# A planner that tells float32 matmul groups from float16 ones, and a first batch planned anew

## The chip, the core and the metric

One core of a Trainium2 chip runs the kernel. The metric is the device time of one execution in microseconds (us); each kernel is given by the median of several executions.

## What is computed

Attention within hash buckets, then a gated two-matrix layer (4 batches, 8 heads, 768 positions, head size 64; 512 model columns, 1536 hidden columns):

```python
q_bits = einsum('bhsd,dk->bhsk', q, proj) > 0      # 6 bits for each query, and for each key
mask   = q_bucket[..., :, None] == k_bucket[..., None, :]
scores = where(mask, q @ k.T / 8, -1e9)
attn   = softmax(scores)
x      = (attn @ v) laid out as (3072, 512)
out    = ((x @ w_a) * (x @ w_b)) @ w_out
```

## The kernel before

**The pieces.** The work is cut into batch `b`, chunk of 256 queries `c` (3 for each batch) and `half` of the heads. Each of these 24 units has eight score tiles. A name such as `s_2_1_0_1_1_0` reads: batch 2, chunk 1, half 0, then head pair, head and row tile. TensorE works in groups of matmuls, and the groups carry the names of the tiles that they write:

- `s` (L740): four matmuls of 384 columns on float32 (fp32r) operands; the scores of one tile, in one of two PSUM buffers with tag `s`. VectorE takes the row maximum `mx` (L752) and adds a constant (`bias`, L759), ScalarE takes the exponent `e` (L767), and with that the PSUM buffer is free.
- `av` (L801): 18 matmuls of 64 columns on float16; weights times values, once the float16 halves `a2` of `e` (L781 on VectorE, L786 on GpSimd) have been transposed by DMA into `at`.
- `px` (L837): four transposes of the normalized output `x` (L828), which then becomes float16 `xT0` (ScalarE, L848) and `xT1` (VectorE, L851).
- `ab` (L885): twelve matmuls of 256 columns on float16; `x @ w_a` or `x @ w_b` for 128 hidden columns. Two such groups fill the one `ab` buffer; ScalarE (`a`, L899) and VectorE (`g`, L907) empty it, and ScalarE and GpSimd split the product into two float32 parts (L914, L917).
- `o` (L927): six matmuls of 512 columns on float32; the product times `w_out`.
- `pk`, `kb`, `ko` and `pq`, `qb`, `qo`: the preparation of keys and of queries: transposes, bit sums (`kb` and `qb` are float32, L513), and bit differences (float16).

**Float32 groups** below are `s`, `o`, `kb` and `qb`; all other groups are called float16 groups, the transposes among them.

**Who sets the order.** Every piece is recorded as an operation of a `Plan` with an engine, a duration in us, a key (its due time in score tiles) and the tiles that it reads and writes. `Plan.issue` then steps through a time of its own: an engine that is free takes, among the operations whose inputs and buffers are there, the one with the lowest key. The instructions are written out in that order, and on the chip each engine runs its own list in order, waiting on semaphores. The choice, at L181:

```python
for o in ready[e]:
    if o.ready <= now and (best is None or (o.key, o.seq) < (best.key, best.seq)) and can(o):
        best = o
```

The keys of batch 0 are tables at the head (L42 to L52): when keys, values and queries are loaded, when the weights `w_a`, `w_b` (`WG0`) and `w_out` (`WO0`) are brought into shape (`raw`, `wab`, `wo_y`, `wo`), and when the first two units of the second layer start (`M0`, `M0_PACE`). Later batches repeat one pattern: 16 score tiles for each 12 rounds of `ab`, `ab`, `o`.

Of the kernel before, what the change touches and what calls it, by code (L numbers as in the profile page):

```python
# [31 lines left out]
NCH = S // CH  # L32
TPC = CH // P

NE, NA, NAT, NO = 3, 2, 2, 2

ACT_CASTS = 8
K_LEAD, Q_LEAD, V_LEAD = 8.0, 2.5, 6.0  # L42
M_LAG = 7.0
K0 = [-12.0, -11.5, -9.5, 6.0]
V0 = [-2.0, -2.0, 5.5, 0.5]
Q0 = [-6.0, 4.5, 9.0, 14.0, 29.0, 31.5]
VS0 = -3.0
WG0 = [11.0, 7.0, 11.5, 14.0, 17.5, 23.5]
S_LAG = -2.5
WO0 = [13.5, 16.0, 36.0]  # L50
M0 = [19.0, 42.5]
M0_PACE = [1.88, 1.33]  # L52
BIG = float(2.0**60)
ESC = float(2.0**14)
# [31 lines left out]
DVE_BESIDE, POOL_BESIDE = 0.5, 0.25  # L86


class Buf:


# [10 lines left out]


class Op:
    __slots__ = ("eng", "dur", "fn", "key", "bufs", "svc", "sbuf", "preds", "succs", "npred", "ready", "seq")


class Plan:
# [4 lines left out]
    def __init__(self):  # L113
        self.ops, self.writer, self.readers = [], {}, {}

    def op(self, eng, dur, fn, key, r=(), w=(), svc=0.0, hold=(), sbuf=False):
        o = Op()
        o.eng, o.dur, o.fn, o.key, o.svc, o.sbuf = eng, dur, fn, key, svc, sbuf
        o.seq = len(self.ops)
        preds = set()  # L120
        for x in r:
            if x in self.writer:
                preds.add(self.writer[x])
            self.readers.setdefault(x, []).append(o.seq)
        for x in w:
            if x in self.writer:
                preds.add(self.writer[x])
            preds.update(self.readers.pop(x, ()))
            self.writer[x] = o.seq
        preds.discard(o.seq)  # L130
        o.preds = preds
        o.bufs = []
        for x in (*r, *w, *hold):
            x = x[0] if isinstance(x, tuple) else x
            if isinstance(x, Buf) and x not in o.bufs:
                o.bufs.append(x)
                x.left += 1
        self.ops.append(o)
        return o

    def issue(self):
# [7 lines left out]
        ready = {e: [] for e in free}  # L149
# [3 lines left out]
        live = {}  # L153
        dma_free = 0.0
        held = set()
        beside = False
        done = 0
        now = 0.0
        events = [0.0]
# [10 lines left out]
        while done < len(ops):  # L170
# [6 lines left out]
            for e in free:  # L177
                if free[e] > now:
                    continue
                best = None  # L180
                for o in ready[e]:  # L181
                    if o.ready <= now and (best is None or (o.key, o.seq) < (best.key, best.seq)) and can(o):
                        best = o
                if best is None:
                    continue
                o = best
# [8 lines left out]
                if e == "DVE":  # L195
                    beside = o.sbuf
                    if o.sbuf and free["POOL"] > now:
                        end += DVE_BESIDE
                elif e == "POOL" and beside and free["DVE"] > now:
                    end += POOL_BESIDE  # L200
                free[e] = end
# [28 lines left out]
def attention_moe(ctx: ExitStack, tc: tile.TileContext, q, k, v, proj, w_a, w_b, w_out, cst, cst_w, out):  # L230
# [288 lines left out]
    def kprep(b, hp, key, tag):  # L519
# [49 lines left out]
        def rows():  # L569
# [2 lines left out]
                bit_rows(psb.t[:, j, :HALF], [(h, tr[h].t[:, 1, cols]) for h in range(2)], exact)  # L572

        op(
            "PE", 1.5 if exact else 0.75, rows, key,
            r=["pjw"] + [(tr[h], x) for h in range(2) for x in ("hi2", "lo")], w=[psb],
        )
        if exact:
            op(
# [26 lines left out]
                    start=True, stop=True,  # L606
                )

        op("PE", 0.35, diffs, key, r=["bits_k", "wbit"], w=[pso])
        for h in range(2):  # L610
            op(
                "ACT", 0.81,
# [7 lines left out]
    def qprep(b, c, half, key, tag):  # L620
# [30 lines left out]
        for h in range(2):  # L651
# [23 lines left out]
                psb.t[:, 0, :CH],  # L675
                [(2 * j + h, trq[h].t[:, j, 1, :]) for j in range(2) for h in range(2)], exact,
            ),
            key, r=["pjw"] + [(trq[h], x) for h in range(2) for x in ("hi2", "lo")], w=[psb],
        )
        if exact:  # L680
            op(
# [25 lines left out]
                    start=True, stop=True,  # L707
                )

        op("PE", 0.25, diffs, key, r=["bits_q", "wbit"], w=[pso])  # L710
        for h in range(2):
            op(
                "ACT", 0.68,
# [7 lines left out]
    def su_state(b, c, half):  # L721
        n = f"{b}_{c}_{half}"
        return dict(
            mx=buf("mx", [P, 4 * TPC], F32, f"mx_{n}", 3),
            bias=buf("bias", [P, 4 * TPC], F32, f"bias_{n}", 3),
            sm=buf("sm", [P, 4 * TPC], F32, f"sm_{n}", 3),
            av=buf("av", [P, 4 * TPC, D], F32, f"av_{n}", 1, pp),
        )

    def qtile(b, c, half, j, h, t, st, key):  # L730
# [6 lines left out]
        def scores():  # L737
# [5 lines left out]
                    )  # L743

        op(
            "PE", 0.72, scores, key, w=[ps],
            r=[(trq, x) for x in ("hi", "hi2", "lo", "hot")] + [(tr, x) for x in ("hi", "hi2", "lo", "pen")],
        )
        mx, bias, sm, av = st["mx"], st["bias"], st["sm"], st["av"]
        op(  # L750
# [58 lines left out]
    def su_end(b, c, half, st, key, tag):  # L809
# [34 lines left out]
        def part(y):  # L844
            return y.t[:, 2 * half : 2 * half + 2, :].rearrange("p j s -> p (j s)")

        op("PE", 0.45, tps, key, r=[x, "csb"], w=[ps], hold=[hi, lo])
        op("ACT", 0.6, lambda: nc.scalar.copy(out=part(hi), in_=ps.t[:, 0]), key, r=[ps], w=[(hi, half)])  # L848
        op(
            "DVE", 0.68,  # L850
# [7 lines left out]
    def moe(b, c, key, pace, alone):  # L858
# [3 lines left out]
        for f in range(NF):  # L862
# [16 lines left out]
            for m in range(2):  # L879

                def first(m=m, f=f, pl=pl):
                    i = 0
                    for wi, xi in ((0, xh), (1, xh), (0, xl)):
                        for cc in range(NC):
                            nc.tensor.matmul(  # L885
                                pl.t[:, m, :CH], lhsT=wt(m, wi, cc, f), rhs=xi.t[:, cc, :],
                                start=i == 0, stop=i == 3 * NC - 1,
                            )
                            i += 1

                j0 = (gr + m) * NC
                op(
                    "PE", 1.31, first, kf, w=[(pl, m)],
                    r=xtok + [(x, j0 + cc) for x in "WL" for cc in range(NC)],
                )
            a = buf("a", [P, CH], F32, f"a_{n}", 1)
# [26 lines left out]
            def second(f=f, g=g):  # L923
# [6 lines left out]
                        )  # L930

            op(
                "PE", 1.42, second, kf + pace * 1.2, w=[po],
                r=[g[0], g[1], (wo[f], 0), (wo[f], 1)],
            )
        for u in range(TPC):
# [83 lines left out]
```

## Time and profile before

| | |
|---|---|
| median of 3 runs | 1012.32 us (1007.96 to 1012.86) |
| the profiled execution | 1012.15 us, of which the span takes 1010.4 us |
| busy: TensorE matmul, weight loads | 936.4 us (93%), 793.3 us (79%) |
| busy: VectorE, ScalarE, GpSimd | 630.5 us (62%), 557.5 us (55%), 456.2 us (45%) |
| chain that ended last, by engine | TensorE 86%, VectorE 7%, ScalarE 3%, issue 2%, DMA 1% |
| chain that ended last, by line | `ab` 37%, `o` 19%, `s` 13%, `av` 9% |

The profile is of one execution. "Busy" counts an engine's instructions; the chain is followed back from the last instruction, at each step to what released it or to the instruction before it on its engine. In the chain view, a row's time runs up to the start of the next row, so that it is the time that a group took of the engine.

### The profile page before, as it was taken

To read this page: it belongs to the slowest core of one execution; us is meant where nothing else is said; L and a number is where in the kernel's file an instruction comes from. 1 tells how busy PE (TensorE), PEld (TensorE's weight loads), DVE (VectorE), ACT (ScalarE), POOL (GpSimd) and SP (SyncE) were. 2 spreads that over 40 slices of the span, in tenths; PEclk is the share of its full clock that TensorE was granted. 3 is DMA by queue.
4 is the path that set the end of the run, shared out by engine and by line. 5 is a ranking of instruction groups with operands and counts; after the bars stand their busy time and mean duration, and the time that the engine had idled before them with its cause. 6 is when DMAs were issued, how large, how long until landed. Compare 5 with 4: busy or idle time off the path is not lost.

```text
span 1010.4 us, 22786 instructions
## 1 busy us (share of the span) xinstructions
PE 936.4 (93%) x9132; PEld 793.3 (79%) x9132; DVE 630.5 (62%) x1135; ACT 557.5 (55%) x1067; POOL 456.2 (45%) x372
## 2 busy tenths in 40 slices
PE   3464679999999999999999999999999999999998
PEld 1243468888888888888888888888888888888886
DVE  4798998777575555567676565557666565555111
ACT  5888865645655554455665555455665554443221
POOL 1033345446554555544555555544545455455211
PEclk9856779999999999999999999999999999999999
DMA  8589956666555445566544565465554455544100
GB/s 286 223 213 208 188 127 139 123 165 149 102 124 116 105 101 131 110 131 152 119 128 106 105 127 109 108 149 137 126 123 103 105 133 103 95 101 95 32 22 21
DMA packets 370154, 127.46 MB, mean 126 GB/s; under 512 B 353920, under 2 KB 362368, under 8 KB 370048
## 3 DMA queue, kind: packets, MB, share of 16 engines
q1 hardware_dynamic: 370048, 126.00, 54.9%
q8 instruction: 72, 1.18, 0.5%
q14 instruction: 34, 0.28, 0.1%
HBM read 44.18 MB, written 6.29 MB: 50 GB/s over the span
## 4 chain that ended last, share of the span: by engine, by line
PE 86%; DVE 7%; ACT 3%; issue 2%; DMA 1%; SPq 0%; POOL 0%; POOLq 0%; DVEq 0%; ACTq 0%
PE ab L885 37%; PE o L927 19%; PE s L740 13%; PE av L801 9%; PE kb L513 2%; PE qb L513 2%; DVE mx L752 1%; PE pk L539 1%; PE px L837 1%; PE pq L644 1%; ACT e L767 1%; DVE wab L370 1%; DVE wab L425 1%; DVE trk L560 1%; PE ko L604 1%
## 5 line engine op out<-in xcount | busy, mean ns | idle before, releaser
L786 POOL TENSOR_TENSOR a<-e,a 128x768 f16<-128x768 f32 x192 | 323.2, 1683 | 322.0 <-DVE a L781 175.9
L885 PE MATMUL ab<-xT,wab 128*128 128x256 f16 x3456 | 413.3, 273 | 0.5 <-DVE bias L759 0.5
L885 PEld LDWEIGHTS <-wab 128*128 128x128 f16 x3456 | 326.4, 98 | 59.4 <-issue 23.3
L767 ACT ACTIVATE e<-s,bias 128x768 f32<-128x768 f32 x192 | 172.7, 899 | 136.5 <-DVE bias L759 125.1
L927 PE MATMUL o<-wo,g 128*128 128x512 f32 x864 | 234.3, 406 | 0.3 <-ACT g L914 0.2
L752 DVE TENSOR_REDUCE mx<-s 128x1 f32<-128x768 f32 x192 | 182.5, 951 | 70.1 <-PE s L740 69.2
L917 POOL TENSOR_TENSOR g<-g,g 128x256 fp32r<-128x256 f32 x144 | 109.0, 757 | 186.1 <-ACT g L914 175.2
L740 PE MATMUL s<-trk,trq 128*128 128x384 f32 x768 | 180.5, 365 | 7.8 <-ACT e L767 6.3
L927 PEld LDWEIGHTS o<-wo,g 128*128 128x128 f32 x864 | 153.4, 189 | 27.6 <-ACT g L914 0.7
L907 DVE SCALAR_TENSOR_TENSOR g<-ab,absc,a 128x256 f32<-128x256 f32 x144 | 69.4, 482 | 158.8 <-ACT a L899 147.1
L801 PEld LDWEIGHTS <-at 128*128 128x128 f16 x3456 | 122.7, 100 | 32.7 <-issue 24.0
L740 PEld LDWEIGHTS s<-trk,trq 128*128 128x128 f32 x768 | 135.5, 198 | 15.7 <-ACT e L767 10.5
L899 ACT ACTIVATE a<-ab,absc 128x256 f32<-128x256 f32 x144 | 68.3, 474 | 131.0 <-PE ab L885 129.9
L801 PE MATMUL av<-vh,at 128*128 128x64 f16 x2304 | 133.8, 196 | 4.8 <-DMA at<-a 4.8
L781 DVE CAST a<-e 128x768 f16<-128x768 f32 x184 | 111.5, 606 | 25.7 <-ACT e L767 19.6
L914 ACT CAST g<-g 128x256 fp32r<-128x256 f32 x144 | 58.1, 404 | 55.9 <-DVE g L907 54.1
L801 PE MATMUL av<-vl,at 128*128 128x64 f16 x1152 | 66.6, 195 | 1.8 <-DVE vl L499 1.8
L714 ACT ACTIVATE trq<-qo,csb 64x512 fp32r<-64x512 f32 x48 | 32.8, 683 | 35.4 <-PE qo L705 34.9
L664 DVE TENSOR_TENSOR trq<-pq,trq 64x512 fp32r<-64x512 f32 x48 | 33.0, 688 | 24.2 <-ACT trq L659 20.7
L555 POOL CAST trk<-trk 64x768 fp32r<-64x768 f32 x32 | 26.7, 833 | 40.3 <-ACT trk L548 39.4
L560 DVE SCALAR_TENSOR_TENSOR trk<-pk,trk 64x768 fp32r<-64x768 f32 x32 | 30.6, 955 | 21.7 <-ACT trk L548 21.2
L654 ACT CAST trq<-pq 64x512 fp32r<-64x512 f32 x48 | 27.8, 580 | 23.0 <-PE pq L644 20.0
(77 smaller groups left out, 670.9 us busy)
## 6 DMA issues: line engine op xcount, KB each, us to landing
rk<-in_k_dram SPq DMA_DIRECT2D x32, 192.0 KB, 3.2
raw_w<-in_moe_w_b_dram SPq DMA_DIRECT2D x12, 512.0 KB, 6.4
raw_w<-in_moe_w_a_dram SPq DMA_DIRECT2D x12, 512.0 KB, 8.2
raw_wo<-in_moe_w_out_dram SPq DMA_DIRECT2D x12, 512.0 KB, 5.3
rq<-in_q_dram SPq DMA_DIRECT2D x96, 64.0 KB, 2.4
vm<-in_v_dram SPq DMA_DIRECT2D x16, 384.0 KB, 3.5
vr<-in_v_dram SPq DMA_DIRECT2D x16, 384.0 KB, 3.6
out_dram<-osb SPq DMA_DIRECT2D x24, 256.0 KB, 2.7
```

Source lines behind the costliest of these rows:

```text
L740: nc.tensor.matmul(ps.t[:, jj, :HALF], lhsT=trq.t[:, j, i, t * P : (t + 1) * P], rhs=tr.t[:, i, jj * HALF : (jj + 1) * HALF], start=i == 0 ...
L752: lambda: nc.vector.tensor_reduce(out=mx.t[:, u : u + 1], in_=halves(ps.t), axis=AX.XY, op=ALU.max, negate=True),
L767: lambda: nc.scalar.activation(flat2(e.t), halves(ps.t), AF.Exp, bias=bias.t[:, u : u + 1], scale=1.0, accum_out=sm.t[:, u : u + 1],),
L781: "DVE", 0.55, lambda: nc.vector.tensor_copy(out=a2.t[:, 0], in_=e.t), key,
L786: lambda: nc.gpsimd.tensor_tensor(out=a2.t[:, 1], in0=e.t, in1=a2.t[:, 0], op=ALU.subtract),
L801: nc.tensor.matmul(av.t[:, u, :], lhsT=at.t[:, a + kt, :], rhs=w.t[:, h, kt, :], start=i == 0, stop=i == 3 * NT - 1,)
L885: nc.tensor.matmul(pl.t[:, m, :CH], lhsT=wt(m, wi, cc, f), rhs=xi.t[:, cc, :], start=i == 0, stop=i == 3 * NC - 1,)
L899: lambda a=a, pl=pl, gr=gr: nc.scalar.activation(a.t, pl.t[:, 0, :CH], AF.Copy, scale=absc[:, b, gr : gr + 1]),
L907: lambda a=a, g32=g32, pl=pl, gr=gr: nc.vector.scalar_tensor_tensor(out=g32.t, in0=pl.t[:, 1, :CH], scalar=absc[:, b, gr + 1 : gr + 2], in ...
L914: op("ACT", 0.41, lambda g=g, g32=g32: nc.scalar.copy(out=g[0].t, in_=g32.t), kf - 8, r=[g32], w=[g[0], "order_g0"])
L917: lambda g=g, g32=g32: nc.gpsimd.tensor_tensor(out=g[1].t, in0=g32.t, in1=f32(g[0].t), op=ALU.subtract),
L927: nc.tensor.matmul(po.t[:, u, :], lhsT=g[gi].t[:, us], rhs=wo[f].t[:, wi * DM : (wi + 1) * DM], start=f == 0 and i == 0, stop=f == NF - 1 ...
```

## The change

The planner gets a flag `wide` for three kinds of groups (`kb`, `s`, `o`; not `qb`). When the last TensorE operation was wide, a wide operation's key counts as 4 lower; a wide operation that follows one that is not costs 0.08 us more. New tokens between TensorE groups: `kb` waits for the `ko` before it, `qb` for the `qo` before it, the `ab` groups stay in the order in which they were recorded, and from its sixth score tile on a unit waits for the `px` of the unit before. The tables of batch 0 get new numbers in four rows (`Q0`, `VS0`, `WG0`, `M0`), and in later batches the values are loaded 5 instead of 6 score tiles ahead. The instructions themselves are the same on every engine, and as many; 14988 rows stand on TensorE before and after.

```diff
+AHEAD = 5
-K_LEAD, Q_LEAD, V_LEAD = 8.0, 2.5, 6.0
+K_LEAD, Q_LEAD, V_LEAD = 8.0, 2.5, 5.0
-VS0 = -3.0
-WG0 = [11.0, 7.0, 11.5, 14.0, 17.5, 23.5]
+VS0 = -5.0
+WG0 = [11.0, 9.0, 11.5, 14.0, 17.5, 23.5]
-M0 = [19.0, 42.5]
+M0 = [18.5, 38.5]
...
+SWITCH, NEAR = 0.08, 4.0
...
                 best = None
+                rank = None
                 for o in ready[e]:
-                    if o.ready <= now and (best is None or (o.key, o.seq) < (best.key, best.seq)) and can(o):
-                        best = o
+                    r = (o.key - (NEAR if wide and o.wide else 0.0), o.seq)
+                    if o.ready <= now and (best is None or r < rank) and can(o):
+                        best, rank = o, r
...
+                elif e == "PE":
+                    if o.wide and not wide:
+                        end += SWITCH
+                    wide = o.wide
...
-            r=["pjw"] + [(tr[h], x) for h in range(2) for x in ("hi2", "lo")], w=[psb],
+            r=["pjw", "turn_k"] + [(tr[h], x) for h in range(2) for x in ("hi2", "lo")], w=[psb],
...
-        op("PE", 0.35, diffs, key, r=["bits_k", "wbit"], w=[pso])
+        op("PE", 0.35, diffs, key, r=["bits_k", "wbit"], w=[pso, "turn_k"])
...
-            "PE", 0.72, scores, key, w=[ps],
-            r=[(trq, x) for x in ("hi", "hi2", "lo", "hot")] + [(tr, x) for x in ("hi", "hi2", "lo", "pen")],
+            "PE", 0.7, scores, key, wide=True, w=[ps],
+            r=[(trq, x) for x in ("hi", "hi2", "lo", "hot")] + [(tr, x) for x in ("hi", "hi2", "lo", "pen")]
+            + [st["before"]] * (u >= AHEAD),
...
-                    "PE", 1.31, first, kf, w=[(pl, m)],
+                    "PE", 1.31, first, kf, w=[(pl, m), "order_first"],
...
-                "PE", 1.42, second, kf + pace * 1.2, w=[po],
+                "PE", 1.4, second, kf + pace * 1.2, wide=True, w=[po],
```

**What moves, first place.** TensorE in the third batch, where the last groups of unit (1, 2) of the second layer stand beside the scores of unit (2, 1, 0). Of each group its first row is shown (`av` has 18 such rows, `ab` twelve, `o` four). Before:

```order
L801 MATMUL av_2_1_0_8166<-vh_2_0_6366,at_2_1_0_0_0_1_8143 128x64
...
L885 MATMUL ab_2_0_0_8241<-xT0_2_0_7704,wab_73 128x256
...
L740 MATMUL s_2_1_0_1_1_0_8261<-trk_2_1_1_6443,trq_2_1_0_1_7764 128x384 x4
...
L801 MATMUL av_2_1_0_8166<-vh_2_0_6366,at_2_1_0_0_1_0_8199 128x64
...
L513 MATMUL qb_2_1_1_8304<-trq_2_1_1_0_8210,pjw_67 56x256
...
L927 MATMUL o_1_2_7224<-wo11_1865,g0_1_2_11_8208 128x512 x2
...
L740 MATMUL s_2_1_0_1_1_1_8323<-trk_2_1_1_6443,trq_2_1_0_1_7764 128x384 x4
...
```

Now:

```order
L814 MATMUL av_2_1_0_8097<-vh_2_0_6192,at_2_1_0_0_1_0_8146 128x64
...
L940 MATMUL o_1_2_7280<-wo10_1692,g0_1_2_10_8167 128x512 x2
...
L752 MATMUL s_2_1_0_1_1_0_8270<-trk_2_1_1_6398,trq_2_1_0_1_7726 128x384 x4
L752 MATMUL s_2_1_0_1_1_1_8277<-trk_2_1_1_6398,trq_2_1_0_1_7726 128x384 x4
...
L814 MATMUL av_2_1_0_8097<-vh_2_0_6192,at_2_1_0_0_1_1_8210 128x64
...
L898 MATMUL ab_2_0_0_8304<-xT0_2_0_7601,wab_73 128x256
...
```

The two score tiles, which stood on either side of `ab`, `av`, `qb` and `o`, stand next to each other behind an `o`. Counted over all rows, a float32 group follows a float16 group 257 times before and 207 times now; of these, 117 and 66 follow an `av`. From the first `ab` on it is 237 and 190, of which 107 and 60 follow an `av`; the 130 that follow another group are 130 still.

**Second place.** VectorE in batch 0, around the output `x_0_0_1` of the first chunk, which the first `ab` needs through `px` and `xT`. Before:

```order
L752 TENSOR_REDUCE mx_0_1_0_1156<-s_0_1_0_0_1_1_1241 128x1
L781 CAST a2_0_1_0_0_0_1_1281<-e_0_1_0_0_0_1_1237 128x768
L425 SCALAR_TENSOR_TENSOR wab_73<-wab_73,wsc4_1203 128x512
L828 TENSOR_TENSOR x_0_0_1_1285<-av_0_0_1_909,r_0_0_1_1105 128x512
L759 TENSOR_SCALAR bias_0_1_0_1164<-mx_0_1_0_1156 128x1
L752 TENSOR_REDUCE mx_0_1_0_1156<-s_0_1_0_1_0_0_1254 128x1
```

Now:

```order
L841 TENSOR_TENSOR x_0_0_1_1272<-av_0_0_1_902,r_0_0_1_1091 128x512
L794 CAST a2_0_1_0_0_0_1_1277<-e_0_1_0_0_0_1_1221 128x768
L436 SCALAR_TENSOR_TENSOR wab_73<-wab_73,wsc4_1242 128x512
L765 TENSOR_REDUCE mx_0_1_0_1145<-s_0_1_0_0_1_0_1231 128x1
L772 TENSOR_SCALAR bias_0_1_0_1149<-mx_0_1_0_1145 128x1
L765 TENSOR_REDUCE mx_0_1_0_1145<-s_0_1_0_0_1_1_1244 128x1
```

`x_0_0_1` moved up, past two `wab`, two `mx`, one `bias` and one `a2` (over all rows ahead of it; two `raw` to `wab` conversions moved ahead of it instead), and one `a2`, one `wab` and one `mx` came between it and the next `bias`. On TensorE the last score tile ahead of the first `ab` was `s_0_1_0_1_0_1` and is now `s_0_1_0_1_0_0`: one tile more stands behind it.

**Third place.** TensorE in the fourth batch, between two rounds that use the one `ab` buffer; now:

```order
L898 MATMUL ab_2_2_4_10918<-xT0_2_2_9727,wab_73 128x256
...
L850 MATMUL px_3_0_0_11000<-csb_64,x_3_0_0_10977 128x128 x4
L752 MATMUL s_3_0_1_1_0_0_11007<-trk_3_3_0_10474,trq_3_0_1_0_10675 128x384 x4
...
L898 MATMUL ab_2_2_5_11018<-xT0_2_2_9727,wab_73 128x256
...
L814 MATMUL av_3_0_1_11038<-vh_3_2_10259,at_3_0_1_0_0_0_10969 128x64
...
```

Only a `px` and an `s` stand between round 4 and round 5 there; before, both groups of round 5 stood right behind a pair of score tiles, and this `px` came behind round 6.

## Rows read from the trace of the kernel before

**Rows 1.** Windows: busy us (x instructions) of each engine, granted clock, DMA share, GB/s.

```profile
0.00:50.00 50.00, 19.04 (x64) 10.48 (x65) 28.75 (x46) 33.73 (x52) 5.15 (x10) 0.93 0.75 257
50.00:147.00 97.00, 59.65 (x472) 45.52 (x472) 88.91 (x148) 79.60 (x138) 36.06 (x21) 0.68 0.81 184
147.00:1000.00 853.00, 851.96 (x8566) 733.36 (x8565) 511.07 (x939) 443.28 (x877) 413.56 (x340) 1.00 0.52 113
```

**Rows 2.** Waits of TensorE's matmuls from 147 us to the end: total, times, longest.

```profile
PE ab L885 <- DVE bias L759: 0.5, 1, 0.5
PE av L801 <- DMA at<-a: 0.3, 1, 0.3
PE o L927 <- ACT g L914: 0.2, 1, 0.2
```

**Rows 3.** The chain that ended last, 160 to 190 us: start, duration, group.

```profile
163.37 0.52 PE av L801 x18
163.90 0.77 PE s L740 x4
164.67 1.32 PE ab L885 x12
165.99 0.70 PE s L740 x4
166.69 1.40 PE o L927 x6
168.09 1.33 PE ab L885 x12
...
169.94 1.31 PE ab L885 x12
...
171.95 0.54 PE av L801 x18
172.49 1.48 PE o L927 x6
...
183.37 0.44 PE pq L644 x4
...
186.54 0.44 PE px L837 x4
```

**Rows 4.** Timeline, 224 to 229 us: the rows of the `ab` buffer.

```profile
224.46 1.48 PE L885 MATMUL ab<-xT,wab 128*128 128x256 f16 x12
...
226.04 0.48 ACT L899 ACTIVATE a<-ab,absc 128x256 f32<-128x256 f32 x1 [0.87 <-PE ab L885]
...
226.62 0.48 DVE L907 SCALAR_TENSOR_TENSOR g<-ab,absc,a 128x256 f32<-128x256 f32 x1
...
227.16 1.47 PE L885 MATMUL ab<-xT,wab 128*128 128x256 f16 x12 [0.47 <-DVE bias L759]
```

**Rows 5.** Timeline, 143 to 148.5 us: the way to the first `ab`.

```profile
142.74 0.74 DVE L425 SCALAR_TENSOR_TENSOR wab<-wab,wsc 128x512 f16<-128x512 f32 x1
...
143.40 0.68 DVE L828 TENSOR_TENSOR x<-av,r 128x512 f32<-128x512 f32 x1
...
144.00 0.14 DVE L759 TENSOR_SCALAR bias<-mx 128x1 f32<-128x1 f32 x1
144.06 0.94 DVE L752 TENSOR_REDUCE mx<-s 128x1 f32<-128x768 f32 x1
...
144.25 0.90 ACT L767 ACTIVATE e<-s,bias 128x768 f32<-128x768 f32 x1
...
145.30 1.59 PE L740 MATMUL s<-trk,trq 128*128 128x384 f32 x4
145.59 0.55 DVE L781 CAST a<-e 128x768 f16<-128x768 f32 x1
...
146.69 2.14 PE L885 MATMUL ab<-xT,wab 128*128 128x256 f16 x9
...
147.99 0.68 DVE L370 SCALAR_TENSOR_TENSOR wab<-raw_w 128x512 int32<-128x512 int32 x1
```

More of the change, by code (lines that the diff above doesn't have):

```diff
@@ L45 @@
 V0 = [-2.0, -2.0, 5.5, 0.5]
-Q0 = [-6.0, 4.5, 9.0, 14.0, 29.0, 31.5]
-VS0 = -3.0
-WG0 = [11.0, 7.0, 11.5, 14.0, 17.5, 23.5]
+Q0 = [-6.0, 4.5, 9.5, 14.0, 29.0, 31.5]
+VS0 = -5.0
+WG0 = [11.0, 9.0, 11.5, 14.0, 17.5, 23.5]
 S_LAG = -2.5
 WO0 = [13.5, 16.0, 36.0]
-M0 = [19.0, 42.5]
+M0 = [18.5, 38.5]
 M0_PACE = [1.88, 1.33]
@@ L104 @@
 class Op:
-    __slots__ = ("eng", "dur", "fn", "key", "bufs", "svc", "sbuf", "preds", "succs", "npred", "ready", "seq")
+    __slots__ = ("eng", "dur", "fn", "key", "bufs", "svc", "sbuf", "wide", "preds", "succs", "npred", "ready", "seq")
 class Plan:
@@ L114, in __init__, with op @@
         self.ops, self.writer, self.readers = [], {}, {}
-    def op(self, eng, dur, fn, key, r=(), w=(), svc=0.0, hold=(), sbuf=False):
+    def op(self, eng, dur, fn, key, r=(), w=(), svc=0.0, hold=(), sbuf=False, wide=False):
         o = Op()
-        o.eng, o.dur, o.fn, o.key, o.svc, o.sbuf = eng, dur, fn, key, svc, sbuf
+        o.eng, o.dur, o.fn, o.key, o.svc, o.sbuf, o.wide = eng, dur, fn, key, svc, sbuf, wide
         o.seq = len(self.ops)
@@ L155, in issue @@
         held = set()
-        beside = False
+        beside = wide = False
         done = 0
@@ L574, in kprep @@
         op(
-            "PE", 1.5 if exact else 0.75, rows, key,
-            r=["pjw"] + [(tr[h], x) for h in range(2) for x in ("hi2", "lo")], w=[psb],
+            "PE", 1.5 if exact else 0.75, rows, key, wide=True,
+            r=["pjw", "turn_k"] + [(tr[h], x) for h in range(2) for x in ("hi2", "lo")], w=[psb],
         )
@@ L677, in qprep @@
             ),
-            key, r=["pjw"] + [(trq[h], x) for h in range(2) for x in ("hi2", "lo")], w=[psb],
+            key, r=["pjw", "turn_q"] + [(trq[h], x) for h in range(2) for x in ("hi2", "lo")], w=[psb],
         )
@@ L708, in diffs @@
                 )
-        op("PE", 0.25, diffs, key, r=["bits_q", "wbit"], w=[pso])
+        op("PE", 0.25, diffs, key, r=["bits_q", "wbit"], w=[pso, "turn_q"])
         for h in range(2):
@@ L723, in su_state @@
         return dict(
+            before=("px", (b * NCH + c) * 2 + half - 1),
             mx=buf("mx", [P, 4 * TPC], F32, f"mx_{n}", 3),
@@ L845, in part @@
             return y.t[:, 2 * half : 2 * half + 2, :].rearrange("p j s -> p (j s)")
-        op("PE", 0.45, tps, key, r=[x, "csb"], w=[ps], hold=[hi, lo])
+        op("PE", 0.45, tps, key, r=[x, "csb"], w=[ps, ("px", (b * NCH + c) * 2 + half)], hold=[hi, lo])
         op("ACT", 0.6, lambda: nc.scalar.copy(out=part(hi), in_=ps.t[:, 0]), key, r=[ps], w=[(hi, half)])
```

## The prediction, made before the changed kernel ran

> **What bounds the kernel now.** I read the windows first, because the page's 93% for TensorE is an average over two stages. Before 147 us TensorE is busy 19.0 of 50 us and then 59.7 of 97 us, while VectorE is busy 88.9 of those 97: here VectorE's list sets the pace, and TensorE runs at a mean granted clock of 0.68. From 147 us on TensorE is busy 852.0 of 853.0 us at a granted clock of 1.00, its upper level of 2.4 GHz, and VectorE only 511 [rows 1]. The waits of TensorE's matmuls confirm it: three waits, 1.0 us in all, over the last 860 us [rows 2]. So from the first `ab` on, the time is the sum of what TensorE's groups take, in whatever order they stand, and a reordering can only pay in two ways: if a group costs a different amount behind another neighbour, or if the start gets shorter.
>
> That first question is answered by the chain view, where a row lasts until the next one starts. The same score tile `s` takes 0.77 us behind an `av` and 0.70 us behind an `ab`; the same `o` takes 1.48 us behind an `av` and 1.40 us behind an `s` [rows 3]. A float32 group that follows an `av` pays 0.07 to 0.08 us; one that follows an `ab` pays nothing that shows. The rows also show a smaller price on the way out: `ab` takes 1.31 us behind an `av`, and 1.32 and 1.33 us behind an `s` and an `o`; `av` takes 0.52 us behind an `ab` and 0.54 us behind an `s` [rows 3]. Leaving float32 costs 0.01 to 0.02 us.
>
> **The terms, with the profiled execution's own 1012.15 us as the base.** That is its span of 1010.4 us and 1.75 us around it, and 0.17 us below the median of the runs shown. No instruction is added or removed, so all terms come from the new order. I count switches from the first `ab` on, since before it TensorE has idle time that hides them.
>
> 1. Entries. Behind an `av` they fall from 107 to 60. 47 x 0.08 = 3.8 us saved; with 0.07 it is 3.3. I take the larger value, which `o` shows. The entries behind other groups stay 130, at no price.
>
> On this the Trainium skill speaks against the change: the table at the head of the page "TensorE: Matmul & The Clock Gate" says that the engine's queue is 64 deep with a partial reorder window, through which weight loads are pulled ahead of matmuls in flight. By that rule the load of a float32 group would hide behind the `av` before it, and this term would be zero. The 0.77 against 0.70 us [rows 3] says that here it doesn't hide fully, so I weigh the rule as a rival only.
>
> 2. Exits. They fall from 237 to 190. 47 x 0.015 = 0.7 us saved (0.5 at 0.01, 0.9 at 0.02).
>
> 3. The single `ab` buffer. The rows of 224 to 227 us show what a round needs: its group `ab` starts at 224.46, `a` and `g` empty the buffer, and the next `ab` starts at 227.16, after TensorE had stood for 0.47 us. Between the two starts lie 2.70 us, of which the group itself takes 1.32, so 1.38 us of other work must stand between two rounds [rows 3, 4]. In the new order I added up the groups that stand between rounds and found five places with less. Three can be worked out from rows: twice a transpose and an `s`, 0.44 + 0.70 = 1.14, and once an `av` and an `s`, 0.52 + 0.77 = 1.29 [rows 3]; in two more a short `ko` or `qo` takes part, and I take the same 1.14 for them as an estimate. The shortfalls are 4 x 0.24 + 0.09 = 1.1 us. The old place at 227 us is gone, which gives 0.5 back. Net 0.6 us lost. From below: if every wait of [rows 2] goes and none comes, 1.0 us is gained. From above: if VectorE and ScalarE are busy with one `mx` (0.94) or one `e` (0.90) [rows 5] when a round at these five places ends, it is some 0.5 us more at each, on average half of one such instruction: 3 us lost.
>
> 4. The start. `x_0_0_1` sets the first `ab`. Ahead of it on VectorE's list stand fewer instructions: two `wab` (0.74 each), two `mx` (0.94), one `bias` (0.14) and one `a2` (0.55) are gone, and two conversions of `raw` (0.68) have come: 4.05 - 1.36 = 2.7 us less [rows 5]. But the way from `x` to the first `ab` is longer. Before, a `bias` followed at once (143.40 to 144.00), then `e` (144.25), the score tile (145.30) and the first `ab` (146.69) [rows 5]. Now an `a2`, a `wab` and an `mx` stand ahead of that `bias`: 0.55 + 0.74 + 0.94 = 2.2 us more. So the first `ab` starts 0.5 us earlier, and one score tile (0.70) that was ahead of it is now behind: 0.2 us lost. Bounds: 2.7 - 0.7 = 2.0 us gained, if the longer way lies beside other work; 2.2 us lost, if VectorE's shorter list is not used because it waits for others. I take the middle, since VectorE is busy 92% of this stretch and its list is what moves [rows 1].
>
> What hides the rest: the new tokens only fix orders between groups of TensorE itself, so they add no wait on the chip. SP's list is the same for its first 44 rows; after that a few weight loads stand one place earlier or later among the loads of keys and queries. The DMA engines are busy 81% of that stretch [rows 1], and I cost the swaps at nothing, because VectorE's list has other work while a load is late; if it ran dry, that would come out of the bounds of term 4. VectorE and ScalarE have 342 and 410 us of room behind 147 us [rows 1]: two adjacent score tiles ask for two `mx` and two `e` in a row, which they can catch up on.
>
> Sum: -3.8 - 0.7 + 0.6 + 0.2 = -3.7 us, so 1012.15 - 3.7 = 1008.4 us. Against the median this is 0.4% less. About 0.5% (5 us) is what a measurement of this kernel can tell from no change, so the likeliest case counts as no change, though I expect the sign to be faster.
>
> **Rivals.**
>
> *The start is shortened for real.* The list ahead of `x_0_0_1` is 2.7 us shorter, and between 50 and 147 us VectorE still waits 97 - 88.9 = 8.1 us [rows 1], some of which other orders may remove. For it: VectorE is the bound there. Against it: VectorE's list is the same for its first 61 rows, so only a part of the start can change. With 2.0 us of term 4 and the 1.0 us of [rows 2] gone it is 1012.15 - 3.8 - 0.7 - 1.0 - 2.0 = 1004.6 us, and up to 1007.2 us with one of these two alone.
>
> *Neighbours don't matter.* The 0.08 us in the chain could be how the profile dates the first matmul of a group, given back elsewhere. Then terms 1 and 2 are zero and 1012.15 + 0.6 + 0.2 = 1013.0 us remains. That is also the time by the skill's rule on the reorder window. Against it: the following rows don't give it back; `o` behind an `s` is 1.40 and the `ab` behind it 1.33 [rows 3].
>
> *Slower: the rounds wait for their buffer.* The lower key pulls score tiles together, and that leaves less between some rounds of `ab`. Apart from the last unit, I find 19 places with less than 2 us between rounds, against 3 before. A round needs 1.38 us with both engines free; if ScalarE starts an `e` (0.90) and VectorE an `mx` (0.94) just then [rows 5], it needs up to 3.2. At 19 places by up to 1.7 us that would be up to 32 us. The point from which it decides: it outweighs the gain of 4.5 us at 0.24 us for each place, and makes the kernel slower by over 0.5% at (5.1 + 4.5 + 0.2) / 19 = 0.5 us for each: 1017.6 us and more. Against it: these engines are busy only 60% and 52% of that stage [rows 1], and some of the 19 places leave 1.9 us.
>
> **How the numbers follow.** The forecast's own case, 1006.5 to 1012 us, gets 0.59; the shorter start 0.25; neighbours that don't matter 0.10; rounds that wait 0.06. Term by term, the ends are -3.8 - 0.9 - 1.0 - 2.0 = -7.7 us (1004.5) and -3.3 - 0.5 + 3 + 2.2 = +1.4 us (1013.5); the upper end needs both bounds at once, so I stop at 1012.6 and leave out part of the third case and the last, and 1004.0 leaves little out below. Faster by over 0.5% begins below 1007.26 us: all of the shorter start and about an eighth of the forecast's case, 0.33. Slower by over 0.5% begins above 1017.4: 0.06. The rest, 0.61, is within 0.5%.
>
> **What would show it.** In the chain of the changed kernel, a score tile behind another score tile or an `o` at 0.70 us, and an `av` followed by one float32 group with the price and the others without; TensorE busy some 848 us from the first `ab` to the same last group; waits of TensorE on VectorE or ScalarE behind 147 us of 1 to 2 us; the first `ab` near 146 us. I am wrong if the first `ab` moves by more than 2 us either way, if TensorE's waits behind it exceed 4 us, or if a float32 group costs 0.77 and 1.48 us whatever stands ahead of it.

## The result, and the profile after

The changed kernel takes 1018.67 us (median of 8 runs, 1015.51 to 1019.53) against 1012.45 us for the kernel before beside it: a ratio of 1.006, with a 95% interval of 1.0046 to 1.0074. It is slower, by 0.6%; the forecast was 1008.4 us, in a range of 1004.0 to 1012.6. The profiled execution of the change took 1016.43 us, 4.28 us more than that of before (1012.15 us), and lies at the low end of its runs. What the traces explain below are these 4.28 us; the 2.2 us between this execution and the median stand in no trace.

The windows of the changed kernel, in the same stretches as [rows 1] (start and end, length, busy us and instructions of TensorE, its weight loads, VectorE, ScalarE and GpSimd, granted clock, DMA share, GB/s):

```profile
0.00:50.00 50.00, 17.87 (x64) 9.79 (x65) 28.80 (x46) 33.58 (x52) 5.15 (x10) 0.78 0.74 257
50.00:147.00 97.00, 62.08 (x468) 47.75 (x467) 89.13 (x146) 79.50 (x138) 35.22 (x20) 0.64 0.84 196
147.00:1000.00 853.00, 847.95 (x8539) 734.67 (x8539) 519.02 (x940) 447.45 (x875) 412.57 (x339) 1.00 0.54 111
```

The last row has changed: TensorE is busy 847.95 of 853 us where it was 851.96, and the granted clock is 1.00 as before. It stands idle for 5.1 us instead of 1.0. In the page's chain ScalarE now has 6% (3% before) and TensorE 82% (86%). The waits of its matmuls from 147 us on, which answer to [rows 2] (line, what it waited for, us in total, times, the longest):

```profile
PE qb L524 <- DVE trq L675: 1.8, 3, 0.7
PE s L752 <- ACT e L780: 1.1, 2, 0.8
PE s L752 <- ACT trq L670: 0.6, 2, 0.4
PE ab L898 <- DVE g L920: 0.6, 2, 0.3
PE av L814 <- DMA at<-a: 0.5, 1, 0.5
PE pk L550 <- ACT trk L624: 0.3, 1, 0.3
PE o L940 <- ACT g L927: 0.3, 1, 0.3
```

Only the fourth of them is the `ab` buffer that the prediction looked at. The first three are new in kind: groups that come before the conversions (`trq`) or the exponentials (`e`) that they need. And the prices of neighbours? The chain from 200 to 222 us, which answers to [rows 3]:

```profile
208.10 1.33 PE ab L898 x12
209.43 0.71 PE s L752 x4
210.14 0.54 PE av L814 x18
210.68 0.78 PE s L752 x4
211.46 1.40 PE o L940 x6
...
219.79 0.70 PE s L752 x4
220.50 1.40 PE o L940 x6
221.89 0.71 PE s L752 x4
```

They are those of before to 0.01 us: `s` takes 0.78 us behind an `av`, 0.70 to 0.71 behind an `ab` or an `o`, and `o` 1.40 behind an `s`.

To see both at once I split each trace from its first `ab` on. **Work** is the sum over TensorE's groups of the price that groups of the same kind and size have between the same neighbours (the 20th percentile over all traces of this study); **waits** are the rest. So the prices of neighbours are put into the work, and the split cannot prove them; where they are at stake below, the time or TensorE's busy time has to show them. The split is good to 1 us or so: with the group ahead alone as the neighbour, the levels change by 1 us, and the difference of the two kernels by 0.1.

| profiled execution | first `ab` at | work | waits | last `o` at |
|---|---|---|---|---|
| before | 146.7 | 851.7 | 5.7 | 1004.1 |
| after | 147.0 | 848.2 | 13.1 | 1008.3 |

So 3.5 us of work were saved and 7.4 us of waits were added; from the last `o` to the end of the execution it is 8.1 us in both. By what waits, of the amounts over 0.06 us: `s` 0.5 before and 3.1 after, `qb` 0.4 and 2.6, `ab` 1.8 and 2.4, `av` 0.6 and 1.3, `pk` 0 and 0.5. The view above shows 4.2 of the 7.4 us (5.2 against 1.0): an `ab` that waits for nothing starts 0.16 us before the modelled end of the group ahead of it, so a start that is late by less leaves no idle time.

One of the new waits, in the timeline of the change (start, length, engine, line, out<-in, and in brackets the idle time before):

```profile
563.18 0.68 DVE L675 TENSOR_TENSOR trq<-pq,trq 64x512 fp32r<-64x512 f32 x1 [0.52 <-ACT trq L670]
...
563.79 1.03 DVE L794 CAST a<-e 128x768 f16<-128x768 f32 x1
...
564.49 0.58 ACT L670 CAST trq<-pq 64x512 fp32r<-64x512 f32 x1
...
564.55 1.47 PE L898 MATMUL ab<-xT,wab 128*128 128x256 f16 x12
564.74 0.94 DVE L765 TENSOR_REDUCE mx<-s 128x1 f32<-128x768 f32 x1
...
565.72 0.15 DVE L772 TENSOR_SCALAR bias<-mx 128x1 f32<-128x1 f32 x1
565.90 0.69 DVE L675 TENSOR_TENSOR trq<-pq,trq 64x512 fp32r<-64x512 f32 x1
...
566.74 0.65 PE L524 MATMUL qb<-trq,pjw 128*56 128x256 f32 x4 [0.72 <-DVE trq L675]
```

`qb` needs the second `trq` of VectorE. Its input from ScalarE is there at 565.07 (564.49 + 0.58), but VectorE works in its order: a cast of `a2`, an `mx` and a `bias` stand ahead, so the `trq` runs from 565.90 to 566.59. TensorE ends its `ab` at 566.02 and has `qb` next in its own order. It stands for 0.72 us, waiting for an engine that is only 61% busy in that stage.

### The profile page after: what moved, and what is told of

Its sections match the earlier page's. It is cut to its first block, busy times and chain, and to the rows that moved or that the text cites. A ratio compares the mean times of both kernels' runs of the same rounds, so it can differ in the third digit from the quotient of the medians.

```text
span 1014.6 us, 22739 instructions
## 1 busy us (share of the span) xinstructions
PE 937.8 (92%) x9132; PEld 799.6 (79%) x9132; DVE 639.2 (63%) x1135; ACT 562.4 (55%) x1067; POOL 455.1 (45%) x372
## 4 chain that ended last, share of the span: by engine, by line
PE 82%; DVE 7%; ACT 6%; DMA 2%; issue 2%; SPq 0%; POOL 0%; POOLq 0%; DVEq 0%; ACTq 0%
PE ab L898 35%; PE o L940 18%; PE s L752 13%; PE av L814 9%; PE kb L524 2%; PE qb L524 1%; PE pk L550 1%; DMA at<-a 1%; ACT trk L624 1%; DVE trq L675 1%; DVE mx L765 1%; ACT e L780 1%; PE px L850 1%; ACT trq L670 1%; PE pq L655 1%
## 5 line engine op out<-in xcount | busy, mean ns | idle before, releaser
L920 DVE SCALAR_TENSOR_TENSOR g<-ab,absc,a 128x256 f32<-128x256 f32 x144 | 69.3, 481 | 149.1 <-ACT a L912 145.9
L752 PEld LDWEIGHTS s<-trk,trq 128*128 128x128 f32 x768 | 140.2, 200 | 27.7 <-ACT e L780 12.7
L794 DVE CAST a<-e 128x768 f16<-128x768 f32 x184 | 112.6, 612 | 40.5 <-ACT e L780 30.4
```

The costliest lines, as they stand in the source:

```text
L752: nc.tensor.matmul(ps.t[:, jj, :HALF], lhsT=trq.t[:, j, i, t * P : (t + 1) * P], rhs=tr.t[:, i, jj * HALF : (jj + 1) * HALF], start=i == 0 ...
L794: "DVE", 0.55, lambda: nc.vector.tensor_copy(out=a2.t[:, 0], in_=e.t), key,
L920: lambda a=a, g32=g32, pl=pl, gr=gr: nc.vector.scalar_tensor_tensor(out=g32.t, in0=pl.t[:, 1, :CH], scalar=absc[:, b, gr + 1 : gr + 2], in ...
```

## Experiments

The letters in each expectation are its own. One table for all; "entries" are float32 groups behind float16 groups from the first `ab` on, counted in the order. Medians and ratios are over several runs, beside runs of the kernel before; the last four columns are of one profiled execution or one plan each. "Idle in the plan" is explained at the last pair of runs; it belongs to a plan, so kernels that reorder a finished plan have none.

| kernel | median us; ratio to before, 95% | entries (behind `av`) | first `ab` | work | waits | idle in the plan |
|---|---|---|---|---|---|---|
| before | 1011.5 to 1012.5 | 237 (107) | 146.7 | 851.7 | 5.7 | 3.5 |
| after | 1018.67; 1.0046 to 1.0074 | 190 (60) | 147.0 | 848.2 | 13.1 | 10.2 |
| e1 no preference | 1015.83; 1.0026 to 1.0053 | 239 (90) | 144.8 | 850.8 | 11.0 | 7.9 |
| e2 old tables | 1026.08; 1.0123 to 1.016 | 190 (64) | 148.5 | 848.8 | 19.6 | 17.2 |
| e3 kept apart | 1019.91; 1.0065 to 1.0099 | 270 (114) | 150.2 | 853.0 | 5.8 | 5.5 |
| e4 longer hops | 1034.04; 1.0204 to 1.0235 | 210 (80) | 152.7 | 849.4 | 23.8 | 51.1 |
| e5 swap on before | 1012.59; 0.9996 to 1.0013 | 213 (31) | 147.2 | 845.8 | 11.5 | |
| e6 swap back | 1016.16; 1.0021 to 1.0046 | 212 (127) | 147.6 | 852.7 | 8.1 | |
| e7 swap on after | 1021.74; 1.0076 to 1.0104 | 185 (22) | 148.1 | 845.8 | 19.4 | |
| e8 tokens alone | 1011.96; 0.9995 to 1.0015 | 250 (105) | 145.9 | 851.9 | 5.8 | 5.5 |
| **e9 swap, last `av` spared** | **1008.37; 0.9949 to 0.9975** | 214 (39) | 147.8 | 846.4 | 6.1 | |
| e10 preferred if rested | 1020.01; 1.0064 to 1.009 | 208 (74) | 145.9 | 849.1 | 16.1 | 15.5 |
| e11 weak preference | 1023.75; 1.0096 to 1.0142 | 203 (83) | 144.7 | 850.3 | 18.6 | 20.8 |
| e12 old tables, no preference | 1013.36; 1.0006 to 1.0029 | 236 (96) | 148.5 | 849.9 | 5.5 | 6.1 |

**e1, e2, e3, e4: the parts of the change.** e1 takes the preference away, e2 puts the old tables back, e3 turns the preference round, with the old tables and without the tokens (entry time and planned times stay those of after), and e4 makes the planner count 0.4 us instead of 0.2 from one engine to another.

e1:

```diff
-SWITCH, NEAR = 0.08, 4.0
+SWITCH, NEAR = 0.08, 0.0
```

e2:

```diff
-K_LEAD, Q_LEAD, V_LEAD = 8.0, 2.5, 5.0
+K_LEAD, Q_LEAD, V_LEAD = 8.0, 2.5, 6.0
...
-Q0 = [-6.0, 4.5, 9.5, 14.0, 29.0, 31.5]
-VS0 = -5.0
-WG0 = [11.0, 9.0, 11.5, 14.0, 17.5, 23.5]
+Q0 = [-6.0, 4.5, 9.0, 14.0, 29.0, 31.5]
+VS0 = -3.0
+WG0 = [11.0, 7.0, 11.5, 14.0, 17.5, 23.5]
...
-M0 = [18.5, 38.5]
+M0 = [19.0, 42.5]
```

e3, with the lines of e2 and the tokens out:

```diff
-SWITCH, NEAR = 0.08, 4.0
+SWITCH, NEAR = 0.08, -4.0
...
```

e4:

```diff
-HOP = 0.2
+HOP = 0.4
```

> The changed kernel with the preference switched off (NEAR 0 instead of 4); tokens and new tables stay. Entries into float32 from the first ab on: 239, of which 90 behind an av (190 and 60 with the preference, 237 and 107 before). Theory W (the preference packs dependent groups too close, and TensorE's new waits of some 7 us outweigh the 3 us that the entries save): the waits fall back to those of before, 1010 to 1013.5 us. Rival T (the new tables of batch 0 cost the time, by their start and by the waits of the first two batches): still 1016 us or more. Rival N (neighbours don't matter and all is waits): as W, no lower than the kernel before.

> The changed kernel with the old tables of batch 0 and the old lead of the values; preference and tokens stay. Entries 190, of which 64 behind an av. W: stays slow, 1015 to 1019 us. T: 1008 to 1011 us, which is the kernel before less the 3 us of the entries and exits.

> The kernel before with the preference turned round: behind a float32 group another float32 group's key counts as 4 higher; old tables, no tokens. Entries 270, of which 114 behind an av. If an entry behind an av costs 0.08 us and an exit 0.02, and the rest is as before: 7 x 0.08 + 33 x 0.02 = 1.2 us more work of TensorE, plus what the new order makes it wait: 1013 to 1016 us. Rival N: the sum of TensorE's groups from the first ab on is the same as before, and only waits differ.

> The changed kernel with HOP 0.4 instead of 0.2 us in the planner, so that it takes results of other engines for ready later and leaves more TensorE work ahead of a dependent group; preference, tokens and new tables stay. Entries 210, of which 80 behind an av. W: the waits behind the first ab fall from 7 us over those of before to 0 to 3 us, and half of the entries' gain is kept: 1009 to 1014 us. T: 1016 us or more.

Without the preference the work goes back to 850.8 us and the waits fall only to 11.0: the preference earns its work, but isn't the only source of waits. e2 speaks against blaming the tables alone: with the old ones and the preference the waits are 19.6 us, 6.5 more than in the kernel after. e3 has the most entries and 4.8 us more work than after, yet the waits of the kernel before; its profiled execution is 4.9 us longer, and of these 3.5 come from its first `ab`, at 150.2 us, and 1.3 from its work. e4 was to give every group more time to get its data; the waits nearly doubled and the start came 5.7 us later. Here longer hops in the planner did not leave room; they made another order. As forecasts of time the four expectations mostly missed: e1 lies between the ranges of W and T, e2 above both, e3 above its 1013 to 1016 us; e4 falls into T's open range, but it changed no table, so it doesn't speak for T.

**e5, e6, e7, e8: neighbours without a new plan, and tokens without anything else.** e5 takes the plan of before as it is and changes only the order in which it is given out; e7 does the same with the plan of after. e6 is the mirror image: a float32 group directly ahead of an `av` goes behind it. e8 is the new source with the preference, the entry time and the new tables and planned times taken back.

```diff
-                o.fn()
+                order.append(o)
...
+    def emit(self, seq):
...
+            while k + 1 < len(seq):
+                k += 1
+                x = seq[k]
+                if o.seq in x.preds or any((b.pool, b.tag) in tags for b in fresh[x]):
+                    break
+                if x.eng == "PE":
+                    if x.kind != "wide":
+                        break
+                    last = k
+            if last is not None:
+                seq[i : last + 1] = seq[i + 1 : last + 1] + [o]
```

e6, for a float32 group `o`:

```diff
+                    if x.eng == "PE":
+                        if x.kind == "av":
+                            seq[i : k + 1] = seq[i + 1 : k + 1] + [o]
```

e8, with the lines of e2 and the planned times of before:

```diff
-SWITCH, NEAR = 0.08, 4.0
+SWITCH, NEAR = 0.0, 0.0
```

(In e5 `o` is an `av`, `wide` are `s`, `o`, `qb` and `kb`; `tags` are the buffers of the `av`, `fresh` those that an operation takes anew.)

> The plan of the kernel before (its tables, times, tokens, and the order on every other engine) stays; only when the list of operations is given out, an av that stands directly ahead of a float32 group is put behind the run of float32 groups that follows it, from the first ab on. By the order, entries into float32 go from 237 to 213 and those behind av from 107 to 31. Theory P (the price by neighbours holds, and the kernel after lost by its new plan, not by its neighbours): TensorE's work falls by 76 x 0.08 = 6.1 us, waits rise by no more than 2 us since every operation keeps its place to within about 1.5 us, the time is 1006 to 1009 us. Theory M (float32 groups side by side make TensorE wait for what stands behind them, however the order is come by): work falls as much, but an av comes up to 1.5 us later and what hangs on it too, waits rise by 6 us or more, the time is 1012 to 1016. Theory N (neighbours do not matter; the fall of work in the kernel after was its shorter planned times): 1011 to 1013.

> The control of the one before: the plan of the kernel before, and a float32 group that stands directly ahead of an av is put behind that av, where the data allow it. By the order, entries behind av go from 107 to 127 while all entries go from 237 to 212, so by the table of prices TensorE's work rises by 20 x 0.08 less 25 exits x 0.015, about 1.2 us. Theory P: 1012.5 to 1014.5 us. Theory M: no gathering, so the waits of the kernel before (5.8 us) stay: 1012 to 1014. Theory N: 1011 to 1013. It tells whether small changes of place alone cost several us: over 1016 would speak for that, against all three.

> The plan of the kernel after with its order on every engine, and the av that still stands directly ahead of a float32 group put behind it. By the order, entries behind av go from 60 to 22, all entries from 190 to 185. Theory P: TensorE's work falls by 38 x 0.08 = 3.0 us, the waits stay near 13 us, so it ends 2 to 3 us under the kernel after, which is 1015.5 to 1017 us, still slower than the kernel before. Theory M: waits rise again by 3 us or more, 1018 to 1021. Theory N: 1018 to 1019.5.

> The kernel before with the new tokens alone (turn_k, turn_q, the px ahead of the scores five tiles on, the order of first halves), the old tables and the old planned times, no preference. By the order 250 entries, 105 of them behind av. Theory P (waits come with any new plan, as in the run without the preference): work 852 to 854 us, waits 8 to 14 us, the time 1014 to 1020. Rival (the tokens only forbid what the plan of before did not do, and cost nothing; it was the new tables and the preference): waits about 6 us, 1012 to 1013.5.

e5 has 76 entries fewer behind `av` and by the split 5.9 us less work. That is the price times the count, so for itself it proves nothing, and the time, 1012.59 us, lies in the ranges of M and N alike. But TensorE is busy for 852.2 us from the first `ab` to the last `o`, where it was 856.1: neighbours matter. (The kernel after has 856.0: one score tile more lies in that stretch, and starts that are late by less than 0.16 us count as busy.) It is no faster, because the waits rise by 5.8 us; P's bound of 2 us was wrong. Here they can be named. The waits of its matmuls from 147 us on begin:

```profile
PE px L868 <- DVE x L859: 3.4, 4, 0.9
PE qb L544 <- DVE trq L695: 0.7, 1, 0.7
```

and one of the four in its timeline:

```profile
363.07 1.65 PE L958 MATMUL o<-wo,g 128*128 128x512 f32 x6
...
364.92 0.34 PE L832 MATMUL av<-vh,at 128*128 128x64 f16 x6
365.30 0.69 DVE L859 TENSOR_TENSOR x<-av,r 128x512 f32<-128x512 f32 x1 [1.79 <-PE av L832]
...
366.14 0.63 PE L868 MATMUL px<-csb,x 128*128 128x128 f32 x4 [0.88 <-DVE x L859]
```

The same place in the kernel before:

```profile
363.54 0.34 PE L801 MATMUL av<-vh,at 128*128 128x64 f16 x6
...
363.71 1.64 PE L927 MATMUL o<-wo,g 128*128 128x512 f32 x6
363.91 0.69 DVE L828 TENSOR_TENSOR x<-av,r 128x512 f32<-128x512 f32 x1 [0.36 <-PE av L801]
...
365.18 0.60 PE L837 MATMUL px<-csb,x 128*128 128x128 f32 x4
```

The last `av` of a half went behind an `o`, 1.4 us later. VectorE forms `x` from all eight `av`, and `px`, next on TensorE, transposes `x`. In the kernel before the `o` covered that way. Four such places are 4.1 of the 5.8 us: 1.04 us each by the split, of which the view shows 0.85.

e6 adds 1.0 us of work for 20 entries less 25 exits, the 1.2 that the prices give, but also 2.4 us of waits, nearly all at an `av` that now comes before its transpose has landed (1.0 us, once) or before VectorE's `x` of the half before is done (1.0 us in three). Its 1016.16 us lie over my bound for small moves that cost nothing. e7 saves 2.4 us of work on the plan of after and pays 6.3 us of waits for it (mainly at `px`, `s` and `qb`); its time lies above all three ranges. e8 takes the time of the kernel before: by themselves the tokens cost nothing, and the idea that any new plan brings waits falls.

**e9: the swap where nobody waits.** The last `av` of a half stays; against e5:

```diff
-        op("PE", 0.55, outs, key, kind="av", r=[at, vh, vl], w=[(av, u)])
+        op("PE", 0.55, outs, key, kind="av" if u < 4 * TPC - 1 else "", r=[at, vh, vl], w=[(av, u)])
```

> As the swap on the kernel before's plan, but the last av of a half (eight a half, the one that the x product of VectorE and then px wait for) keeps its place. By the order 214 entries, 39 of them behind av (31 in the swap, 107 before). Theory W (an av is free to move only where nobody waits for it; the four px waits of 1.04 us each were the whole loss of the swap): TensorE's work falls to about 846.4 us, the waits to 11.6 - 4.1 = 7.5 us, and with the same start the time is 1007.5 to 1009.5 us, under the kernel before by 0.25 to 0.45%. Theory M (gathering float32 groups makes new waits wherever it is done): others take their place, 1011 to 1013.5 us.

The same place in its timeline:

```profile
363.25 0.34 PE L832 MATMUL av<-vh,at 128*128 128x64 f16 x6
363.43 1.64 PE L958 MATMUL o<-wo,g 128*128 128x512 f32 x6
363.63 0.69 DVE L859 TENSOR_TENSOR x<-av,r 128x512 f32<-128x512 f32 x1 [0.36 <-PE av L832]
...
364.91 0.60 PE L868 MATMUL px<-csb,x 128*128 128x128 f32 x4
```

`x` now runs beside the `o`, and `px` follows without a wait. Work 846.4 us, waits 6.1, 1008.37 us: a ratio of 0.9962 to the kernel before (0.9949 to 0.9975). It is faster than both kernels, by the gain that the change was to bring, without its plan, and it lies in Theory W's range. Here the time itself shows the price, which the split could not: with the same instructions, from the first `ab` to the last `o` (147.8 to 1000.2 us) it takes 852.4 us where the kernel before takes 857.4, though the view shows 0.7 us more of waits. That is 5.7 us for 68 entries fewer behind `av` and 23 exits fewer; at 0.08 and 0.015 us they would make 5.8.

**e10: a preference that asks for rest.** In the kernel after, a float32 group is preferred only if its data and buffers have been ready for 1.0 us of the planner's time.

```diff
-SWITCH, NEAR = 0.08, 4.0
+SWITCH, NEAR, LATE = 0.08, 4.0, 1.0
...
+        def rested(o):
+            new = [(b.pool, b.tag) for b in o.bufs if b not in held]
+            return max([o.ready, *(freed.get(k, 0.0) for k in new)]) + LATE <= now
...
-                    r = (o.key - (NEAR if wide and o.wide else 0.0), o.seq)
+                    r = (o.key - (NEAR if wide and o.wide and rested(o) else 0.0), o.seq)
```

> The kernel after, but a float32 group is preferred beside another only when its data and its buffers have been ready, in the planner's time, for 1.0 us; otherwise the planner takes the lowest key as before. By the order 208 entries, 74 of them behind av (190 and 60 in the kernel after). Theory S (the preference starts groups at the very moment that the planner believes their data to be there, and the chip is some tenths later): the waits on casts and exps (qb on trq, s on e and trq, pk, kb: 6 to 7 of the 13 us) fall by half or more, to 6 to 9 us in all, work rises by 14 x 0.08 = 1.1 us to about 849.5, and with the start of the kernel after the time is 1013 to 1016.5 us. Rival (the waits come from the new tables and the reordering, wherever a group stands): waits 11 to 16 us, 1017 to 1021 us.

The theory behind it fell; the time lies in the rival's range, the waits (16.1) at its upper end. Those of `s` and `qb` did fall, from 5.7 to 3.1 us, but those of `ab` rose from 2.4 to 8.9; the waits of its matmuls begin:

```profile
PE ab L903 <- DVE g L925: 5.0, 6, 1.7
PE qb L529 <- DVE trq L680: 0.9, 2, 0.5
```

This is the single `ab` buffer of the slower rival: it decides here, not in the kernel after.

**e11, e12: what the plan itself says.** A look into the planner gave one more theory. The plan dates every group in its own time, and there too TensorE stands idle when nothing on its list may start. Without the 0.08 us that the plan adds for entries, that is 3.5 us from the first `ab` on in the kernel before and 10.2 in the kernel after. (The expectations below say 9.2, and 16.4 and 5.9 for two others: there 0.08 us was taken off for `qb` as well, for which the plan adds nothing. The table has 17.2 and 6.1.) For the plans that had run until then, the idle time in the plan and the waits on the chip stand in the same order (e3 and e8 level with the kernel before on the chip); only e4, which dates its hops longer, has far more in the plan than on the chip. Two plans that had not run were chosen by it.

e11, with the planned times of before:

```diff
-SWITCH, NEAR = 0.08, 4.0
+SWITCH, NEAR = 0.0, 1.0
...
```

e12, with the lines of e2:

```diff
-SWITCH, NEAR = 0.08, 4.0
+SWITCH, NEAR = 0.08, 0.0
```

> The kernel after with a preference of 1.0 place instead of 4.0, no extra time for an entry, and the planned times of before; its tokens and tables stay. By the order 203 entries, 83 of them behind av. In the planner's own time TensorE stands idle for 20.8 us from the first ab on (before 3.5, after 9.2 without its entry times, the old tables with the preference 16.4). Theory G (a plan's waits on the chip follow the idle time that the plan itself holds, and are not misjudged durations): waits of 20 us or more on the chip, work 850 to 851.5, and with the start of the kernel after 1025 to 1031 us. Rival (what was lost lies in the strength of the preference, so a quarter of it loses less than all of it): waits 8 to 12, 1014 to 1018 us.

> The tokens and the shorter planned times of the kernel after with its extra time for an entry, but the old tables and no preference. By the order 236 entries, 96 of them behind av; the plan holds 5.9 us of idle TensorE from the first ab on and sets the first ab 3.0 us later than in the kernel before. Theory G: waits 6 to 9 us, work about 851, the first ab at 148 to 150, 1013 to 1017 us. Rival (any new plan brings 10 us of waits or more): 1017 to 1022 us.

The waits came out at 18.6 and 5.5 us, for 20.8 and 6.1 us in the plans: near the plans and far from the rivals, but both a little under what Theory G expected (20 or more, 6 to 9). So the order is not strict: e2 waits longer than e11 with less idle time in its plan, and e12 has the fewest waits with more than the kernel before. The time of e11 is 1.3 us below the range, since its first `ab` came 2.3 us earlier than that of the kernel after. A quarter of the preference, with the planned times of before and no entry time, costs more than all of it. The waits of its matmuls begin:

```profile
PE ab L898 <- DVE g L920: 6.8, 9, 1.7
PE s L752 <- ACT e L780: 1.5, 3, 0.7
PE ab L898 <- DVE bias L772: 1.4, 3, 0.7
```

With e1, e2 and e12 the change is now taken apart, all four with the tokens and the new planned times, waits in us of one execution each:

| | no preference | preference 4.0 |
|---|---|---|
| old tables | 5.5 (e12) | 19.6 (e2) |
| new tables | 11.0 (e1) | 13.1 (after) |

The preference adds 14.1 us of waits to the old tables; the new tables take 6.5 of these back, and alone would add 5.5. With neither, e12 is back within 0.2% of the kernel before, so the loss comes from these two, and their parts don't add up. Why a new order waits where it does was followed at single places only. That a greedy planner which takes another group first at one place has other groups ready later on, while its list for every engine is then fixed, fits all of this; no run shows it by itself.

## Why the prediction was wrong, step by step

- **Entries and exits** (-3.8 and -0.7 us) were right. The work fell by 3.5 us, and it holds one score tile (0.70 us) more than before, which the prediction counted under the start: -4.2 against -4.5. Counts times prices had to give this; that the prices hold in the time itself is shown by e9.
- **Neighbours don't matter**, the rival by the rule of the Trainium skill's page "TensorE: Matmul & The Clock Gate" (the table at its head, on the reorder window), is refuted: by e9's time, and by `s` at 0.78 and 0.71 us in the chain of the change. It is the price of zero that falls. A load is pulled ahead in these traces, but only beside one matmul: before and after, the first weight load of an `s` or `o` begins 2 to 3 ns (median) after the start of the last matmul ahead of it, behind `av` as behind `ab`, and takes 0.19 us. That last matmul lasts 0.27 us in an `ab` and 0.19 us in an `av`, by the profile's modelled ends: 0.08 us less to hide behind, which is the price. No run here changes that length alone, so this is the reading that fits.
- **The single `ab` buffer** (+0.6 us net) was right in size, in part by luck: the waits of `ab` rose from 1.8 to 2.4 us. The two that the view names (0.32 us at 280.15 and 0.26 at 794.16 us) stand at rounds where more than 1.38 us of other work lay in between, and nothing had been priced there. At the five places that the sum priced at 1.1 us (rounds that begin at 151.29, 301.91, 418.98, 562.72 and 779.65 us) the `ab` starts 0 to 0.24 us later than one that waits for nothing, 0.7 us in all. The slower rival, 0.5 us at each of 19 places, did not happen in the kernel after. The measured time lies where that rival put it (1017.6 us and more), but through other waits.
- **What hides the rest** is the step that failed, and with it the premise that behind the first `ab` the time is the sum of the groups "in whatever order they stand". I costed the adjacent score tiles at nothing, since VectorE and ScalarE "have 342 and 410 us of room behind 147 us" and "can catch up", and the tokens, since they "only fix orders between groups of TensorE itself". The tokens do cost nothing (e8). But what I took for a few adjacent tiles was a new plan for all engines, and waits of `s`, `qb`, `av` and `pk` rose by 6.0 us (and those of other groups by 0.8) at places that I had not looked at, where the sum has zero. Room over a stage is no cover for one place in it: `qb` at 566.74 us waited for an engine that is 61% busy, because that engine had three other instructions first in its order. My own bound, +3 us, was made for the five places of the `ab` buffer only.
- **The start** (+0.2 us, within -2.0 and +2.2): the first `ab` was to come 0.5 us earlier and came 0.3 us later; with the one tile more behind it that is 1.0 us. The net direction was right, the way of the first `ab` was not.
- The sum on the profiled execution: +0.3 - 3.5 + 7.4 = +4.2 us, against 4.28 measured and -3.7 forecast. Of the three signs of being wrong one came: TensorE's waits behind the first `ab` were to stay under 4 us, and the view of waits shows 5.2 (4.7 of them on VectorE and ScalarE, where 1 to 2 were expected). A sum beside the forecast doesn't come out either: for the shorter start "with one of these two alone" the terms give 1006.3 or 1006.9 us, not 1007.2; nothing else hangs on it.

What stays open is why the runs of the change lie 2.2 us over its profiled execution at the median while those of the kernel before agree with theirs; e3 and e11 show the same, with 2.9 and 2.1 us.

## What to carry to other kernels

Where a planner sets the order, a rule about neighbours can change the order everywhere: before counting the saving, list how long the plan itself lets the bounding engine stand, before and after (here 3.5 and 10.2 us). In this kernel the switch cost was better saved behind the plan, by swapping two neighbours where nobody waits for the one that moves back: that gave 0.4%, and one `av` in eight had to be left alone. Average room on an engine says nothing about a single wait on it.

## What the runs showed of the hardware that I had not expected

The price of an entry adds up: 68 entries fewer behind `av` in e9 shortened TensorE's busy time between the first `ab` and the last `o` from 856.1 to 850.7 us, 0.08 us each. And VectorE's cast of `a2` took 1.03 us at 563.79, where [rows 5] show 0.55: half a us more ahead of the `trq` that `qb` waited for. GpSimd was at work when it began, until 564.41, and the cast ended 0.41 us after that. It is so throughout: of the 368 such casts in the traces of before and after, the 279 that met no GpSimd instruction took 0.52 to 0.56 us, and all 26 over 0.9 us lay beside one; of the 75 that began while GpSimd worked, 62 ended 0.41 to 0.42 us after it did. In all, these casts took 112.6 us of VectorE after and 111.5 before.
